# Attention with two gated MLPs on one core: the order of the first loads, the rest scores and the warm-up products

## The chip, the cores and the metric

One core of a Trainium2 chip runs the whole program. The metric is the device time of one execution in microseconds; lower is better. The engines are TensorE (PE, with its weight loads as PEld), VectorE (DVE), ScalarE (ACT), GpSimd (POOL) and SyncE (SP, which issues nearly all transfers here). PE writes into PSUM, from where ACT and DVE read. Each engine works through its own instructions in program order.

## What is computed

Three stages follow one another; all inputs and outputs are float32 or wider. Only the first is touched by the change.

```python
# q, k, v: (4 batches, 12 heads, 448, 64)
scores = scale * q @ k.T - log(448)
attn = 1 / (1 + exp(-scores))             # a sigmoid, no row sum
x = attn @ v                              # heads side by side: (4, 448, 768)
x = moe(x, ...)                           # gated MLP: in 768 -> 1024, over positions, out 512 -> 768
out = moe2(x, ...)                        # the second gated MLP
```

## The kernel before

The attention part treats the 48 heads in 12 groups of four (`attention`, L318). A group's q and k are loaded as 128 partitions (four heads by 32 rows t), each with 14 consecutive positions c of 64 values (`load_qk`, L323). DVE turns 32x32 blocks of them so that the 64 values of a head lie on 32 partitions in two halves (`turn`, L363): `tq` from q, `tk` from the first 12 positions of k, `tr` from the last two. So a group's 448 keys fall into three blocks of 128 and a rest of 64. For the three blocks each operand is split into a rounded part and what remains (`high` and `low`), and a score block (`scores`, L442) is three products by two halves by four heads, 24 in all. Block (0,0), the very first, is made of unsplit operands and uses two value banks beside one score buffer, so that it can start early.

The rest keys of two groups n and n+1 share a block (`scores_rest`, L469): it needs `tq` and `tr` of both groups, unsplit, and its sigmoid goes into one tile for both.

A score block takes two of the three buffers of `ps_att` (two PSUM banks each). ACT weighs them (`weigh`, L435: sigmoid, one instruction for a pair of heads) into a tile that is the moving operand of the value products (`values`, L490), with the stationary operand from `vt` (blocks) or `vr` (rests). A group's values for a pair x of heads add up over its four blocks in one bank, and `gather` (L504) copies the sum away on DVE when the last is in.

The values are loaded by `load_v` (L332): `vt` holds the 12 first positions of the rows t, three positions per block of 32 partitions, for four heads; four DMAs, one per 32 partitions. `vr` (L349) holds the rests, four DMAs more.

The order of work is written out by hand. `units` (L530) lists the score blocks; the loop at L575 issues at step s block s and then the value products that `sums` names for the step. For a pair of groups n, m the order is (n,0), (n,1), (n,3), (n,2), (m,0), (m,1), (m,2), where 3 is the rest of both groups; for the first pair L537 swaps it to (0,0), (0,1), (0,2), (0,3), and the rest is then the last of group 0's value products (`last_of`, L487). At step 0 group 1 is turned (L581). At steps 3 and 6 a later group is turned, at steps 0 and 4 ACT makes the rounded parts of a group (`high`), at 1 and 5 DVE makes the remainders (`low`). `belt.tick` (L589) moves the weight conversions on by a stage each: a load by SP, five operations on DVE (L170 to L188), a cast on ACT (L201), a difference on DVE (L203). In the first steps the first conversion's DVE part is issued at step 1 and its cast at step 2, behind that step's sigmoids.

Ahead of the loop (L565 to L574) stand the loads of groups 0 and 1, products of an identity with itself that keep PE at work while the loads run (L573), and the turning of group 0.

Of the kernel before, what the change touches and what calls it, by code (L numbers as in the profile page):

```python
# [26 lines left out]
def tile_sigmoid_attention_two_gated_mlps(  # L27
# [32 lines left out]
    nc = tc.nc  # L60
    B, H, S, D = q.shape
# [6 lines left out]
    TC = S // 32  # L68
# [30 lines left out]
    def av_bank():  # L99
        return ps_av.tile([P, 512], F32, tag="av", name="av")  # L100
# [217 lines left out]
    def attention(apool, epool, ps_att, done):  # L318
        G = H // 4
        NG = B * G  # L320
        raws, turned, ops, vs, att, avp = {}, {}, {}, {}, {}, {}

        def load_qk(n, xs="kq"):  # L323
            b, i = divmod(n, G)
            hs = slice(4 * i, 4 * i + 4)
            for x in xs:
                t = apool.tile([P, TC * D], F32, tag=f"in{x}", name=f"in{x}", bufs=2)
                src = {"k": k, "q": q}[x][b, hs].rearrange("h (t c) d -> (h t) (c d)", c=TC)
                nc.sync.dma_start(out=t, in_=src)
                raws.setdefault(n, {})[x] = t  # L330

        def load_v(n):  # L332
            b, i = divmod(n, G)
            vs[n] = vt, vr = (
                epool.tile([P, 4, 3, D], F32, tag="v", name="vt", bufs=3),
                epool.tile([P, 2, D], F32, tag="vr", name="vr", bufs=3),
            )
            src = v[b, 4 * i:4 * i + 4].rearrange("h (t c) d -> t h c d", c=TC)
            for e in range(4):
                ts = slice(32 * e, 32 * e + 32)  # L340
                nc.sync.dma_start(
                    out=vt[ts].rearrange("p h c d -> p h (c d)"),
                    in_=src[:, :, 3 * e:3 * e + 3].rearrange("t h c d -> t h (c d)"),
                )
            later["rows"] = lambda: load_v_rest(n, vr, src)
            if n > 0:
                later.pop("rows")()

        def load_v_rest(n, vr, src):  # L349
            for e in range(4):  # L350
                ts = slice(32 * e, 32 * e + 32)
                h = 2 * ((e // 2 + n) % 2)
                hs = slice(h, h + 2)
                nc.sync.dma_start(out=vr[ts], in_=src[:, hs, 12 + e % 2])

        def turn_keys(tk, k):
            for j in range(2):
                nc.vector.transpose(
                    out=tk[:, j].rearrange("p (c e) t -> p c e t", c=3),
                    in_=k[:, j, :12].rearrange("p (e c) d -> p c e d", c=3),  # L360
                )

        def turn(n):  # L363

            tk = apool.tile([P, 2, 12, 32], F32, tag="tk", name="tk", bufs=1)
            tr = apool.tile([P, 2, TC - 12, 32], F32, tag="tr", name="tr", bufs=2)
            tq = apool.tile([P, 2, TC, 32], F32, tag="tq", name="tq", bufs=2)
            at = raws.pop(n)
            k, q = [at[x].rearrange("p (c j d) -> p j c d", c=TC, j=2) for x in "kq"]
            turned[n] = [t.rearrange("p j c t -> p (j c t)") for t in (tk, tr, tq)]  # L370
            ops[n] = (
                apool.tile([P, 2, 6 * P], F32R, tag="opk", name="opk", bufs=2),
                apool.tile([P, 2, 2 * S], F32R, tag="opq", name="opq", bufs=2),
            )
            if n > 1:
                turn_keys(tk, k)
                nc.vector.transpose(out=tq, in_=q)
                nc.vector.transpose(out=tr, in_=k[:, :, 12:])
                return
            if n == 1:  # L380
                nc.vector.transpose(out=tq, in_=q)
                high(n, (1,), nc.vector.tensor_copy)
                low(n, (1,))
                nc.vector.transpose(out=tr, in_=k[:, :, 12:])
                turn_keys(tk, k)
                high(n, (0,), nc.vector.tensor_copy)
                low(n, (0,))
                return

            def some_k(r):  # L390
                nc.vector.transpose(out=tk[:, :, 4 * r:4 * r + 4], in_=k[:, :, r:12:3])
                return 0, slice(r * P, (r + 1) * P)

            def some_q(j):
                nc.vector.transpose(out=tq[:, j], in_=q[:, j])
                return 1, slice(0, S), slice(j, j + 1)

            qs = some_q(0), some_q(1)
            for x in qs:
                high_part(n, *x)  # L400
            for j in range(2):
                nc.vector.transpose(out=tk[:, j, :4], in_=k[:, j, :12:3])
            ks = some_k(1), some_k(2)
            for x in ks:
                high_part(n, *x)
            for x in qs + ks:
                low_part(n, *x)
            nc.vector.transpose(out=tr, in_=k[:, :, 12:])
# [7 lines left out]
        def high_part(n, i, cols, js=slice(0, 2), copy=nc.scalar.copy):  # L416
            t, hi, _ = views(n, i, cols, js)
            copy(out=hi, in_=t)

        def low_part(n, i, cols, js=slice(0, 2)):  # L420
            t, hi, lo = views(n, i, cols, js)
            nc.vector.tensor_tensor(out=lo, in0=t, in1=raw(hi), op=ALU.subtract)

        def high(n, parts=(0, 1), copy=nc.scalar.copy):
            for i in parts:
                high_part(n, i, slice(0, (3 * P, S)[i]), copy=copy)

        def low(n, parts=(0, 1)):
            for i in parts:
                low_part(n, i, slice(0, (3 * P, S)[i]))  # L430
# [53 lines left out]
            att[n, 3] = att[n + 1, 3] = a = epool.tile([P, 4, S], F32, tag="ar", name="ar", bufs=1)  # L484
            weigh(a, pairs(sc))

        def last_of(n):  # L487
            return 2 if n else 3

        def values(n, r, x):  # L490
            if r == 0:
                avp[n, x] = av_bank()
            vt, vr = vs[n]
            at = REST * ((x + n) % 2)
            ps = slice(at, at + REST)
            for o in range(2):
                h = 2 * x + o
                nc.tensor.matmul(  # L498
                    avp[n, x][o * D:(o + 1) * D, :S],
                    vt[:, h, r] if r < 3 else vr[ps, o], att[n, r][:, h] if r < 3 else att[n, r][ps, h],  # L500
                    start=(r == 0), stop=(r == last_of(n)),
                )

        def gather(n, x):  # L504

            b, i = divmod(n, G)
            y = chunk_of(b, 2 * i + x)
            o = avp.pop((n, x))[:, :S].rearrange("p (c t) -> p t c", c=TC)

            def back(at, t0, t1, c0=0, c1=TC):  # L510
                dst = y[:, at:at + (t1 - t0) * (c1 - c0)]
                nc.vector.tensor_copy(
                    out=dst.rearrange("p (t c) -> p t c", t=t1 - t0), in_=o[:, t0:t1, c0:c1]
                )

            if b % 2 == 0:
                back(0, 0, 32)
            else:
                t, c = divmod(3 * P, TC)
                back(SPAN, 0, t)  # L520
                back(SPAN + t * TC, t, t + 1, 0, c)
                back(S, t, t + 1, c, TC)
                back(S + TC - c, t + 1, 32)
# [3 lines left out]
        units, sums = [], {}  # L527
        for n in range(0, NG, 2):
            m, at = n + 1, len(units)
            units += [(n, 0), (n, 1), (n, 3), (n, 2), (m, 0), (m, 1), (m, 2)]  # L530
            both = lambda n, r: [(n, r, 0), (n, r, 1)]
            todo = (
                [(n, 0, 0)], [(n, 0, 1), (n, 1, 0)], [(n, 1, 1)] + both(n, 3), both(n, 2),
                both(m, 0), both(m, 3) + [(m, 1, 0)], [(m, 1, 1), (m, 2, 0)], [(m, 2, 1)],
            )
            if n == 0:
                units[2:4] = units[3:1:-1]  # L537
                todo = [both(0, r)[::-1] for r in range(4)] + list(todo[4:])
            for s, x in enumerate(todo, at + 1):
                sums.setdefault(s, []).extend(x)  # L540
        U = len(units)
# [17 lines left out]
        def weigh_up(s):  # L559
            for n, r, x in sums.get(s, ()):  # L560
                values(n, r, x)
                if r == last_of(n) and n < NG - 1:
                    gather(n, x)

        load_qk(0, "qk")  # L565
        load_qk(1, "q")
        load_v(0)
        load_qk(1, "k")
        later.pop("rows")()
        belt.tick(1)  # L570
        warm = av_bank()
        for _ in range(10):
            nc.tensor.matmul(warm[:, :P], ident, ident, start=True, stop=True)  # L573
        turn(0)  # L574
        for s in range(U + 2):  # L575
            p, step = divmod(s, 7)
            score(s)
            weigh_up(s)
            n = 2 * p + (1 if step < 2 else 2 if step < 6 else 3)
# [10 lines left out]
            if step in (0, 4):  # L590
                n = 2 * p + 2 + step // 4
# [516 lines left out]
```

## Time and profile before

| | us |
|---|---|
| median of 3 runs (lowest, highest) | 556.52 (556.45, 557.28) |
| the profiled execution, its own time | 556.21 |
| its span, first to last instruction | 554.4 |
| PE busy | 549.1 |
| DVE busy | 368.1 |
| ACT busy | 231.5 |

The rows below come from that one profiled execution; times in them are from the start of its span. PE records overlap, since products are pipelined, so a block's own length is the distance to the next block in the chain. "Idle before" is time in which the engine did nothing ahead of an instruction, with what released it. "issue" is time in which the engine waited for nothing that the profile shows. In the table of stretches, the DMA share is the mean busy share of the core's 16 DMA engines; packets in flight together can bring it above 1.

### The profile page before, as it was taken

The numbers are of one execution on the slowest core, as the hardware profiler recorded it, in microseconds if no ns is written. First come the engines' busy times: TensorE is split into PE (matmuls) and PEld (weight loads), VectorE is DVE, ScalarE is ACT, GpSimd is POOL, SyncE is SP. The second block draws the span as 40 slices with busy tenths as digits, with TensorE's granted clock in tenths as the row PEclk, the third lists the DMA queues.
The fourth block names the chain that finished last, engine by engine and source line by source line (L and its number), as shares of the span: only waits on it lengthen the run. The fifth ranks groups of instructions, "written<-read, shape, count | busy, mean of one in ns | idle before, by whom it ended". The sixth has DMA issues, their size and how long they took to land.

```text
span 554.4 us, 9199 instructions
## 1 busy us (share of the span) xinstructions
PE 549.1 (99%) x3472; PEld 437.0 (79%) x3472; DVE 368.1 (66%) x839; ACT 231.5 (42%) x388; POOL 32.7 (6%) x62
## 2 busy tenths in 40 slices
PE   8999999999999999999999999999999999999997
PEld 6444444444799898898998889998999899989886
DVE  6879999997689699999864977951542264224311
ACT  5778778786353262361443156310320041113101
POOL 0000000000110100300100011000100020011000
PEclk9999999999999999999999999999999999999999
DMA  7777677653044265453445534200400032003003
GB/s 246 195 175 224 191 211 200 159 109 73 2 135 141 62 169 120 121 148 102 145 153 129 147 112 125 70 0 9 78 14 0 9 58 36 1 15 60 11 1 114
DMA packets 96892, 56.45 MB, mean 102 GB/s; under 512 B 67536, under 2 KB 84048, under 8 KB 96848
## 3 DMA queue, kind: packets, MB, share of 16 engines
q1 hardware_dynamic: 96704, 55.60, 38.7%
q8 instruction: 27, 0.44, 0.4%
q10 hardware_dynamic: 144, 0.26, 0.1%
q14 instruction: 17, 0.14, 0.1%
HBM read 44.83 MB, written 11.01 MB: 101 GB/s over the span
## 4 chain that ended last, share of the span: by engine, by line
PE 98%; DMA 1%; SPq 0%; issue 0%; DVE 0%
PE t L685 17%; PE t L639 17%; PE av L498 13%; PE sc L771 10%; PE sc L461 9%; PE t L705 6%; PE av L771 5%; PE av L705 3%; PE sc L705 3%; PE sc L781 3%; PE t L867 3%; PE av L867 3%; PE sc L479 2%; PE av L781 2%; PE t L781 2%; DMA vt<-in_v_dram 1%
## 5 line engine op out<-in xcount | busy, mean ns | idle before, releaser
L437 ACT ACTIVATE a<-sc,small 128x896 f32<-128x896 f32 x71 | 67.7, 1008 | 20.4 <-PE sc L461 20.4
L498 PE MATMUL av<-a,vt 128*64 128x448 f32 x288 | 62.9, 553 | 0.4 <-DMA vt<-in_v_dram 0.4
L648 DVE BATCH_NORM_STATS2 st<-vr 128x6 f32<-128x512 f32 x28 | 19.4, 694 | 65.7 <-ACT vr L645 65.7
L461 PEld LDWEIGHTS sc<-opq,opk 32*128 32x128 f32 x840 | 38.6, 183 | 25.5 <-issue 10.8
L645 ACT ACTIVATE vr<-t 128x512 f32<-128x512 f32 x28 | 16.7, 598 | 92.3 <-PE t L639 88.5
L461 PE MATMUL sc<-opq,opk 32*128 32x448 f32 x840 | 53.3, 380 | 0.0
L498 PEld LDWEIGHTS av<-a,vt 128*64 128x64 f32 x288 | 17.2, 136 | 32.4 <-issue 27.9
L639 PE MATMUL t<-vh,xh 128*128 128x512 f32 x112 | 41.5, 391 | 0.0
L715 DVE SCALAR_TENSOR_TENSOR gt<-t,bb 128x448 f32<-128x448 f32 x16 | 10.9, 682 | 45.5 <-PE t L705 45.5
L723 ACT CAST gh<-u 128x448 fp32r<-128x448 f32 (+1 forms) x16 | 8.6, 540 | 71.5 <-DVE u L719 71.5
L650 POOL TENSOR_SCALAR st<-st 128x1 f32<-128x1 f32 x28 | 11.0, 391 | 466.6 <-DVE st L649 466.6
L639 PE MATMUL t<-vh,xl 128*128 128x512 f32 x98 | 38.1, 389 | 0.0
L685 PE MATMUL t<-xh,uh 128*128 128x448 f32 x96 | 34.8, 363 | 0.0
L685 PE MATMUL t<-xh,ul 128*128 128x448 f32 x96 | 34.8, 362 | 0.0
L685 PE MATMUL t<-xl,uh 128*128 128x448 f32 x96 | 34.6, 360 | 0.0
L705 PE MATMUL t<-sh,v 128*128 128x448 f32 x112 | 32.8, 362 | 0.0
L639 PE MATMUL t<-vl,xh 128*128 128x512 f32 x84 | 32.7, 389 | 0.0
L182 DVE SCALAR_TENSOR_TENSOR f<-w,f 128x256 uint32<-128x256 uint32 x72 | 30.7, 426 | 2.5
L188 DVE SCALAR_TENSOR_TENSOR f<-w,f 128x256 int32<-128x256 int32 x72 | 30.6, 425 | 2.4
L685 PE MATMUL t<-xh,vl 128*128 128x448 f32 x96 | 29.7, 363 | 0.0
L177 ACT ACTIVATE g<-w 128x256 f32<-128x256 f32 x48 | 20.1, 432 | 19.4 <-DMA w<-in_moe_w_out_dram 9.7
L667 ACT CAST v<-vr 128x512 fp32r<-128x512 f32 x24 | 14.9, 621 | 30.6 <-DVE vr L659 30.6
(211 smaller groups left out, 1291.2 us busy)
## 6 DMA issues: line engine op xcount, KB each, us to landing
w<-in_moe_w_in_dram SPq DMA_DIRECT2D x48, 256.0 KB, 3.5
w<-in_moe_w_out_dram SPq DMA_DIRECT2D x24, 256.0 KB, 3.0
inq<-in_q_dram SPq DMA_DIRECT2D x12, 448.0 KB, 6.4
ink<-in_k_dram SPq DMA_DIRECT2D x12, 448.0 KB, 5.7
vt<-in_v_dram SPq DMA_DIRECT2D x48, 96.0 KB, 6.1
out_dram<-y SPq DMA_DIRECT2D x48, 56.0 KB, 1.9
flat<-f SPq DMA_DIRECT2D x18, 128.0 KB, 1.7
w<-flat SPq DMA_DIRECT2D x12, 192.0 KB, 2.4
```

The source lines that it names most:

```text
L177: nc.scalar.activation(g, high.bitcast(F32), AF.Square)
L182: nc.vector.scalar_tensor_tensor(out=f.bitcast(U32), in0=low.bitcast(U32), scalar=29, in1=f.bitcast(U32), op0=ALU.logical_shift_right, op1 ...
L188: nc.vector.scalar_tensor_tensor(out=f, in0=high, scalar=-0x40000000, in1=f, op0=ALU.bitwise_and, op1=ALU.bitwise_or)
L437: nc.scalar.activation(a[:, dst], src[..., :S], AF.Sigmoid, bias=bias_s, scale=scale)
L461: nc.tensor.matmul(banks[h][:, :S], opk[ps, x, o:o + P], opq[ps, y, S * j:S * (j + 1)], start=(t == 0), stop=(t == len(todo) - 1), tile_po ...
L498: nc.tensor.matmul(avp[n, x][o * D:(o + 1) * D, :S], vt[:, h, r] if r < 3 else vr[ps, o], att[n, r][:, h] if r < 3 else att[n, r][ps, h], ...
L639: nc.tensor.matmul(ps[:, :FF], a, w, start=(c == 0 and n == 0), stop=(c == self.kc - 1 and n == 2),)
L685: nc.tensor.matmul(ps[:, :S], w, a, start=(c == 0 and n == 0), stop=(c == self.kc - 1 and n == 2),)
L705: nc.tensor.matmul(ps[:, :S], a, w, start=(n == 0), stop=(n == len(todo) - 1))
L771: nc.tensor.matmul(self.o[m][:, :n_cols], w, a, start=(not second and i == 0 and n == 0), stop=(second and i == KF - 1 and n == 2),)
L781: nc.tensor.matmul(ps[:, :cols.stop - cols.start], a, w, start=(not second and i == 0 and n == 0), stop=(second and i == KF - 1 and n == 2),)
L867: nc.tensor.matmul(ps[:, :FF], x, w[:, c], start=(c == 0 and n == 0), stop=(c == KD - 1 and n == 2),)
```

## The change

The four value DMAs of a group go by head instead of by 32 partitions: each fills all 128 partitions with 768 bytes of one head, read from four strided pieces of 32 rows. The first loads are issued in the order q0, k0, values of 0, q1, k1, rests of 0. In the first pair of groups the rest scores take the third place, as in all other pairs, and the third key block the fourth; the value products follow, so that block 2 is the last of group 0 too and `last_of` goes. Turning group 1 makes all transpositions first, and then the rounded parts and remainders of q and of k. There are eleven identity products in place of ten.

```diff
@@ -335,13 +335,13 @@
                 epool.tile([P, 4, 3, D], F32, tag="v", name="vt", bufs=3),
                 epool.tile([P, 2, D], F32, tag="vr", name="vr", bufs=3),
             )
+            for h in range(4):
+                src = v[b, 4 * i + h].rearrange("(t c) d -> t (c d)", c=TC)[:, :12 * D]
+                nc.sync.dma_start(
+                    out=vt[:, h].rearrange("p c d -> p (c d)"),
+                    in_=src.rearrange("t (e f) -> e t f", e=4),
+                )
             src = v[b, 4 * i:4 * i + 4].rearrange("h (t c) d -> t h c d", c=TC)
-            for e in range(4):
-                ts = slice(32 * e, 32 * e + 32)
-                nc.sync.dma_start(
-                    out=vt[ts].rearrange("p h c d -> p h (c d)"),
-                    in_=src[:, :, 3 * e:3 * e + 3].rearrange("t h c d -> t h (c d)"),
-                )
             later["rows"] = lambda: load_v_rest(n, vr, src)
             if n > 0:
                 later.pop("rows")()
@@ -379,12 +379,11 @@
                 return
             if n == 1:
                 nc.vector.transpose(out=tq, in_=q)
-                high(n, (1,), nc.vector.tensor_copy)
-                low(n, (1,))
                 nc.vector.transpose(out=tr, in_=k[:, :, 12:])
                 turn_keys(tk, k)
-                high(n, (0,), nc.vector.tensor_copy)
-                low(n, (0,))
+                for x in (1, 0):
+                    high(n, (x,), nc.vector.tensor_copy)
+                    low(n, (x,))
                 return
 
             def some_k(r):
@@ -484,9 +483,6 @@
             att[n, 3] = att[n + 1, 3] = a = epool.tile([P, 4, S], F32, tag="ar", name="ar", bufs=1)
             weigh(a, pairs(sc))
 
-        def last_of(n):
-            return 2 if n else 3
-
         def values(n, r, x):
             if r == 0:
                 avp[n, x] = av_bank()
@@ -498,7 +494,7 @@
                 nc.tensor.matmul(
                     avp[n, x][o * D:(o + 1) * D, :S],
                     vt[:, h, r] if r < 3 else vr[ps, o], att[n, r][:, h] if r < 3 else att[n, r][ps, h],
-                    start=(r == 0), stop=(r == last_of(n)),
+                    start=(r == 0), stop=(r == 2),
                 )
 
         def gather(n, x):
@@ -534,8 +530,7 @@
                 both(m, 0), both(m, 3) + [(m, 1, 0)], [(m, 1, 1), (m, 2, 0)], [(m, 2, 1)],
             )
             if n == 0:
-                units[2:4] = units[3:1:-1]
-                todo = [both(0, r)[::-1] for r in range(4)] + list(todo[4:])
+                todo = [both(0, r)[::-1] for r in (0, 1, 3, 2)] + list(todo[4:])
             for s, x in enumerate(todo, at + 1):
                 sums.setdefault(s, []).extend(x)
         U = len(units)
@@ -559,17 +554,16 @@
         def weigh_up(s):
             for n, r, x in sums.get(s, ()):
                 values(n, r, x)
-                if r == last_of(n) and n < NG - 1:
+                if r == 2 and n < NG - 1:
                     gather(n, x)
 
         load_qk(0, "qk")
-        load_qk(1, "q")
         load_v(0)
-        load_qk(1, "k")
+        load_qk(1, "qk")
         later.pop("rows")()
         belt.tick(1)
         warm = av_bank()
-        for _ in range(10):
+        for _ in range(11):
             nc.tensor.matmul(warm[:, :P], ident, ident, start=True, stop=True)
         turn(0)
         for s in range(U + 2):
```

## Rows read from the trace of the kernel before

**Rows 1.** The page: PE's busy time, and the chain that ended last by engine.
```profile
PE 549.1 (99%) x3472; PEld 437.0 (79%) x3472; DVE 368.1 (66%) x839; ACT 231.5 (42%) x388; POOL 32.7 (6%) x62
...
PE 98%; DMA 1%; SPq 0%; issue 0%; DVE 0%
```

**Rows 2.** The chain in order of time: start us, us, what.
```profile
9.60 1.72 PE av L498 x8
...
14.40 1.69 PE sc L479 x32
...
16.09 1.65 PE av L498 x8
...
17.75 1.43 PE sc L461 x20
...
19.18 0.91 PE av L498 x8
...
20.09 1.74 PE sc L461 x19
...
23.49 1.71 PE sc L461 x19
...
27.01 1.42 PE sc L461 x21
...
49.19 1.42 PE sc L461 x21
```

**Rows 3.** Timeline of PE: start us, us, line, operation, tiles, forms, count, idle before.
```profile
1.35 4.63 PE L573 MATMUL av<-ident 128*128 128x128 f32 x20 [1.35 <-POOL ident masks.py:199]
...
6.18 0.69 PE L461 MATMUL sc<-tq,tk 32*128 32x448 f32 x2 [0.20 <-DVE tk L402]
...
17.68 0.48 PE L461 MATMUL sc<-opq,opk 32*128 32x448 f32 x4
...
20.02 0.47 PE L461 MATMUL sc<-opq,opk 32*128 32x448 f32 x2
```

**Rows 4.** PE's waits over the span: total us, times, longest us.
```profile
PE av L498 <- DMA vt<-in_v_dram: 0.4, 1, 0.4
```

**Rows 5.** Timeline of ACT, 8 to 23.6 us.
```profile
16.23 0.41 ACT L201 CAST vh<-f 128x256 fp32r<-128x256 f32 x1 [1.53 <-DVE f L188]
...
16.54 1.91 ACT L437 ACTIVATE ar<-sc,small 128x896 f32<-128x896 f32 x2
...
19.28 1.91 ACT L437 ACTIVATE a<-sc,small 128x896 f32<-128x896 f32 x2 [0.84 <-PE sc L461]
```

**Rows 6.** Timeline of DVE, 3 to 16.3 us.
```profile
4.03 1.17 DVE L395 STREAM_TRANSPOSE tq<-inq 128x448 f32<-128x448 f32 x2 [3.15 <-DMA inq<-in_q_dram]
...
5.81 0.51 DVE L402 STREAM_TRANSPOSE tk<-ink 128x128 f32<-128x128 f32 x2 [0.61 <-DMA ink<-in_k_dram]
...
8.83 1.07 DVE L381 STREAM_TRANSPOSE tq<-inq 128x896 f32<-128x896 f32 x1
...
15.77 0.42 DVE L188 SCALAR_TENSOR_TENSOR f<-w,f 128x256 int32<-128x256 int32 x1
```

**Rows 7.** Timeline of SP, the queue that issues the loads.
```profile
2.10 2.03 SPq L341 DMA_DIRECT2D vt<-in_v_dram  x4
...
8.76 0.43 SPq L162 DMA_DIRECT2D w<-in_moe_w_in_dram  x1
```

**Rows 8.** Stretches: us; busy of PE, PEld, DVE, ACT, POOL; clock, DMA share, GB/s.
```profile
1.50:5.00 3.50, 3.50 (x17) 3.50 (x18) 0.97 (x2) 0.99 (x3) 0.00 (x0) 1.00 0.91 322
...
5.00:5.50 0.50, 0.50 (x4) 0.50 (x4) 0.20 (x1) 0.50 (x2) 0.00 (x0) 1.00 1.00 403
...
5.50:6.00 0.50, 0.48 (x3) 0.18 (x1) 0.19 (x1) 0.30 (x1) 0.00 (x0) 1.00 0.96 328
...
6.00:6.50 0.50, 0.32 (x4) 0.32 (x8) 0.50 (x3) 0.00 (x0) 0.00 (x0) 1.00 1.16 260
...
27.00:49.20 22.20, 22.20 (x246) 10.41 (x244) 17.51 (x42) 17.31 (x23) 0.00 (x0) 1.00 0.73 190
```

## The prediction

> **What bounds the kernel now.** I read the page's busy table and its chain first: TensorE (PE) is busy for 549.1 of 554.4 us, and PE makes up 98% of the chain that ended last, DMA 1% [rows 1]. So only a change in when PE works can move the time, and PE sits idle for little more than 5 us in all, most of it before the first and after the last product. Next the chain in order of time over the first 27 us [rows 2]: from 9.60 us on PE goes from one block to the next without a gap. A full score block of four heads takes 1.43 us, a block of four value products 1.65, the rest scores 1.69, the rest values 0.91. Two score blocks stand out, 1.74 at 20.09 and 1.71 at 23.49: 0.3 us more each for the same products. The PE timeline tells why [rows 3]: at 20.02 two products start instead of four, and the other heads begin 0.3 us later. They wait for a score buffer. There are three (ps_att, two banks each), a block takes two, and ScalarE (ACT) must weigh what is in them first. The release comes 1.06 us after ACT starts on a pair (19.28 to 20.34), so 1.16 after the last score, while the rest values between the two blocks last only 0.91. PE's one named wait in this stretch is 0.4 us for the values of group 0 [rows 4]. Last come ACT and VectorE (DVE) [rows 5, 6], since both work in program order, and SP with the transfers [rows 7, 8].
>
> Times below are of the profiled execution: span 554.4, its own time 556.21, which is 0.3 below the median of the three runs, 556.52.
>
> **The change, part by part.**
>
> *The loads of group 0.* SP issues q0, k0, the four value loads, then q1, k1. The values start about 0.5 us earlier at SP (the four take 2.03 us from 2.10 on now [rows 7]), q1 moves from just ahead of them to about 3.7, and k1 and all behind it keep their places. The data moves in order: from 1.5 to 5.0 us 1127 KB (3.5 us at 322 GB/s), so q0 and k0 (917 KB) are through at about 4.5 and the values follow [rows 8].
>
> What the new value load costs no row shows. It moves the same bytes (393 KB in pieces of 768 B), but its source is an outer count of 4 pieces against 128 partitions, while every load of before has 32 or 128 as the outer count on both sides. If the pieces are dealt to all sixteen DMA engines, the lower bound is the rate at the start of the values, 328 GB/s [rows 8]: 1.2 us. If they are dealt by the outer count that both sides share, only four engines work. One busy engine moved 328/(16 x 0.96) = 21.4 GB/s there, 260/(16 x 1.16) = 14.0 in the next half microsecond, 25.2 with the large pieces of q and k before. Four engines then need 4.6 us (3.9 to 7.0). I take four at 21.4: a source of 4 and a destination of 128 have no finer outer cut in common. The Trainium skill (DMA: Bandwidth & Descriptors, "Why a DMA increments its semaphore by 16 and not by 1") says that a DMA runs on the largest number of engines up to 16 that divides both slowest dimensions: 4 here, so the rule gives the sum I take; no load in this trace tests it. Against it the skill (SBUF — State Buffer, "Door 1: The DMA port swizzle") says that a transfer into 32 partitions reaches half of the ports and one into 128 all; the trace agrees (403 GB/s for q and k, 260 among the values), and by this alone the load gets cheaper and the sum is that of the first rival.
>
> On those four engines the values end at 4.5 + 4.6 = 9.1, a sixteenth of q1 (28.7 KB at 25.2 GB/s, 1.1 us) at 10.2, of k1 at 11.35. The first load landed 0.7 us after its bytes were through (458 KB at about 3.3, VectorE starts on it at 4.03 [rows 6]); with that lag q1 lands at 10.9 and k1 at 12.05. The values land near 9.8: PE's wait for them stays, 0.2 us longer. The order by head does not help, as heads 2 and 3 are used first and loaded last.
>
> *VectorE.* The nine operations of turn(1) are the same, in another order: tq, the rests tr, the keys, then the copies and differences. They run without a gap from 8.83 on now, and the first weight conversion, right behind them, is done at 16.19 [rows 6]. With q1 there at 10.9, tq ends at 11.97, and tr starts at 12.1 where it would at 9.9: everything behind is late by **2.2 us**, the conversion done at 18.4. Its own input does not set this: SP issues it at 8.76 [rows 7], and behind q1 and k1 (through at 11.35) its 16 KB per engine are there by 13, long before VectorE comes to it.
>
> *Rest scores third.* The same products, so PE's busy time is the same; what moves is who waits for a buffer. The blocks become (0,0), (0,1), rest, (0,2), (1,0). The rest needs tq and tr of group 1, now 12.4 instead of 11.2: PE loses about 0.6 there, after the part that needs only group 0. The short rest values now stand ahead of (1,0), so that block has the buffer wait: its second buffer is free 1.06 us after ACT starts on (0,2). On ACT that pair stands behind one cast of L201, which waits for the conversion on VectorE. Today the same cast holds up the rest scores' pair (16.23, then 16.54 [rows 5]), behind which a full value block of 1.65 hides it. That cover is gone: the short values hide 0.91. So (1,0) gets its second buffer at 18.4 + 0.04 (to the cast) + 0.31 (to the weighing) + 1.06 = 19.8.
>
> From there I add blocks: (1,0) ends at 19.8 + 1.49 = 21.3 (1.49 is what the block at 20.09 took from its own release at 20.34 [rows 2, 3]), values 22.95, (1,1) without its wait 24.4, values 26.05, (1,2) without its wait 27.45. Before, that block ended at 25.20 [rows 2]: **2.25 us later**. The two removed waits (0.6) are in this sum, and PE runs without gaps from there to the end, so nothing is won back. A longer or shorter value wait in group 0 is swallowed by the wait at (1,0).
>
> *The eleventh identity product and last_of.* Ten products are 20 records about 0.22 us apart, ending at 5.98, and PE idles 0.20 before the first score [rows 3]. Two records more fill that gap and cost 0.05 to 0.25; it too ends in the wait at (1,0), so nothing. The granted clock is 1.00, the 2.4 GHz level, in every stretch [rows 8], so there is none to win. last_of only fixes which product closes the sum.
>
> The sum: 556.21 + 2.25 = **558.5**. Bounds: the four engines' 3.9 to 7.0 us move it by -0.7 to +2.4; a lag of 0.1 to 1.3 instead of 0.7 (k0: through at 4.5, landed before 5.8 [rows 6]) by -0.6 to +0.6; together, both ends at once being unlikely, +0.9 to +4.
>
> **The rivals.**
>
> *All sixteen engines carry the load* (not slower). q1 lands before 8.8, VectorE has no gap, the conversion is done at 16.19 as now. Values start 0.24 earlier (after ACT's first pair). The buffer wait at (1,0) still comes: ACT starts on (0,2) at 16.54, release 17.60, while PE arrives at 16.73 (9.36 + 1.65 + 1.69 + 1.65 + 1.43 + 0.91 and some hundredths); (1,0) ends at 19.09 against 19.18, values 20.74, (1,1) 22.17, values 23.83, (1,2) 25.26 against 25.20. So +0.1 (-0.75 if the cast is out of the way, +0.6 if q1 is a little late): 556.3, from 555.5 to 556.8. For it speak the fall in rate among 32-partition loads; against it the outer count of 4. It decides if q1 lands before 9 us.
>
> *Four engines, and later loads late too.* Per group those engines then carry 4.6 us of values, 2.3 of q and k, 1.6 of weights (five per pair of groups), 0.2 of rests: 8.7 of the 11.1 us that a group lasts (from group 2's first score block at 27.01 to group 4's at 49.19 are two [rows 2]). At 14.0 GB/s the values alone take 7.0 and the engines are full: from there loads fall behind and PE waits in most groups, 0.3 to 0.5 us in ten of them, 3 to 5 us more: 562. Against it speaks that the mean DMA share of that stretch is 0.73 [rows 8], so that there is room on the engines that the values leave.
>
> **How the numbers follow.** Four engines 0.64, sixteen 0.28, four with late loads 0.08. About 0.2% (1.1 us) is what a measurement of this kernel can tell from no change. Of the first case I give 0.09 to less than that; so slower is 0.64 - 0.09 + 0.07 = 0.62, same 0.09 + 0.26 + 0.01 = 0.36, faster 0.02. The range takes the four-engine case to +3.9 (560.1) and most of the sixteen-engine case (556.2); the likeliest case alone is 557.1 to 560.1.
>
> **What would show it.** In the changed profile: a DMA share near 0.25 for some 4 us from about 5 us on, q1's transposition starting at 10 or later instead of 8.83, the cast of L201 past 18, (1,0) split into two starts with a gap of 2 us, (1,1) and (1,2) at 1.43 without the split start. If the share stays near 1 while the values load and tq starts at 8.83, the first rival holds. If the value rows of later groups show PE waiting for vt, the second.

## The result and the profile after

The changed kernel takes **559.88 us** (559.53 to 560.91, 6 runs); the kernel before, measured beside it, 556.75 (556.45 to 558.56, 6 runs). The ratio is 1.0053 [1.0038, 1.0068], so 0.5% slower. The profiled execution took 559.84 us with a span of 558.1; before it was 556.21 and 554.4. So 3.6 to 3.7 us were lost between the two profiles, and 3.1 between the medians, where 2.25 were forecast.

The page gives the first reading: PE's busy time, and the shares of the chain that ended last.

```profile
PE 550.9 (99%) x3474; PEld 438.2 (79%) x3474; DVE 368.0 (66%) x839; ACT 231.2 (41%) x388; POOL 32.6 (6%) x62
...
PE 96%; DMA 1%; DVE 1%; SPq 1%; ACT 0%; issue 0%
```

PE is still the bound, but 4% of the chain, some 20 us, now belongs to others, against 2% in [rows 1]. PE's waits over the span, apart from 1.3 us for the identity at the start that both kernels have (total us, times, longest us):

```profile
PE sc L460 <- ACT a L436: 1.0, 1, 1.0
PE av L494 <- ACT a L436: 0.8, 1, 0.8
PE av L494 <- DMA vt<-in_v_dram: 0.5, 1, 0.5
```

All three lie in the first 22 us, and they are new or longer than the 0.4 of [rows 4]. The chain in order of time (start us, us, what) shows how they hang together:

```profile
5.57 8.08 DMA ink<-in_k_dram
...
13.67 0.03 DVE tr L382
...
19.36 0.43 DVE f L188
...
19.82 0.41 ACT vh L201
20.22 0.92 ACT a L436
...
21.18 1.50 PE sc L460 x17
...
24.33 1.43 PE sc L460 x21
...
27.41 1.44 PE sc L460 x18
28.85 1.81 PE av L494 x12
```

Read from the end: the scores of (1,2) are done at 28.85, where they were done at 25.20 (23.49 + 1.71) in [rows 2], 3.65 us later; that is the whole loss of the span, so nothing is won or lost behind it. (1,1) and (1,2) take 1.43 and 1.44: the two buffer waits of [rows 2] are gone. (1,0) waits for ACT's weighing (20.22), that for the cast of L201 (19.82), that for the conversion on DVE, and DVE turned q1 late (its row follows) and then waited another 0.1 us for a k1 that landed 8.08 us after its issue. PE, from the first values to (1,0) (start us, us, line, operation, tiles, forms, count, idle before):

```profile
10.10 0.94 PE L494 MATMUL av<-a,vt 128*64 128x448 f32 x2 [0.82 <-ACT a L436]
11.57 1.69 PE L494 MATMUL av<-a,vt 128*64 128x448 f32 x6 [0.54 <-DMA vt<-in_v_dram]
13.19 2.58 PE L478 MATMUL sc<-tq,tr 32*64 32x448 f32 x32
...
19.69 0.47 PE L460 MATMUL sc<-opq,opk 32*128 32x448 f32 x2
21.18 1.50 PE L460 MATMUL sc<-opq,opk 32*128 32x448 f32 x22 [1.03 <-ACT a L436]
```

The value products come a head at a time, two records each. The first start at 10.10. The row names ACT, but the pair that they read was weighed by 9.19 (ACT's two instructions of 8.03 us, 1.16 together), so I read the wait as one for the values of head 2; head 3, loaded last, keeps PE until 11.57. The rest scores' row is 2.58 long, where the timeline of before has 1.76 for them (at 14.34): the rest keys of group 1 are turned only at 13.67 + 0.31. At 19.69 two products of (1,0) start, and the other heads 1.5 us later. DVE and SP tell why, here q1's transposition on DVE:

```profile
12.44 1.11 DVE L381 STREAM_TRANSPOSE tq<-inq 128x896 f32<-128x896 f32 x1 [4.25 <-DMA inq<-in_q_dram]
```

and the loads at SP:

```profile
1.63 2.48 SPq L340 DMA_DIRECT2D vt<-in_v_dram  x4
4.15 1.38 SPq L329 DMA_DIRECT2D inq<-in_q_dram  x1
5.57 0.43 SPq L329 DMA_DIRECT2D ink<-in_k_dram  x1
```

VectorE idles 4.25 us for q1, where it had no gap in [rows 6]. SP's issue of q1 alone took 1.38 us, against 0.39 to 0.43 for the other three q and k loads of groups 0 and 1. Last the stretches (us; busy of PE, PEld, DVE, ACT, POOL; clock, DMA share, GB/s):

```profile
4.50:6.50 2.00, 2.00 (x13) 1.88 (x16) 2.00 (x7) 1.63 (x4) 0.00 (x0) 1.00 0.28 75
6.50:8.00 1.50, 1.50 (x23) 1.25 (x20) 1.50 (x5) 0.19 (x1) 0.00 (x0) 1.00 0.89 209
27.00:49.20 22.20, 22.20 (x244) 10.37 (x240) 17.68 (x40) 17.32 (x23) 0.00 (x0) 1.00 0.67 210
```

From 4.5 to 6.5 us the share is 0.28, close to 4 of 16 engines, at 75 GB/s, where [rows 8] show 0.96 to 1.16 and 260 to 403 GB/s for the half microseconds from 5 to 6.5. Then q1 and k1 fill the other engines.

### The profile page after: what moved, and what is told of

Read it like the earlier page. It is cut to its first block, busy times and chain, and to the rows that moved or that the text cites. A ratio compares the mean times of both kernels' runs of the same rounds, so it can differ in the third digit from the quotient of the medians.

```text
span 558.1 us, 9192 instructions
## 1 busy us (share of the span) xinstructions
PE 550.9 (99%) x3474; PEld 438.2 (79%) x3474; DVE 368.0 (66%) x839; ACT 231.2 (41%) x388; POOL 32.6 (6%) x62
## 4 chain that ended last, share of the span: by engine, by line
PE 96%; DMA 1%; DVE 1%; SPq 1%; ACT 0%; issue 0%
PE t L679 17%; PE t L633 17%; PE av L494 12%; PE sc L765 10%; PE sc L460 8%; PE t L699 6%; PE av L765 5%; PE av L699 3%; PE sc L699 3%; PE sc L775 3%; PE t L861 3%; PE av L861 3%; PE sc L478 2%; PE av L775 2%; PE t L775 1%; DMA ink<-in_k_dram 1%
## 5 line engine op out<-in xcount | busy, mean ns | idle before, releaser
L639 ACT ACTIVATE vr<-t 128x512 f32<-128x512 f32 x28 | 16.7, 598 | 92.5 <-PE t L633 88.7
L709 DVE SCALAR_TENSOR_TENSOR gt<-t,bb 128x448 f32<-128x448 f32 x16 | 10.9, 682 | 45.6 <-PE t L699 45.6
L644 POOL TENSOR_SCALAR st<-st 128x1 f32<-128x1 f32 x28 | 10.9, 390 | 470.3 <-DVE st L643 470.3
L177 ACT ACTIVATE g<-w 128x256 f32<-128x256 f32 x48 | 19.8, 432 | 17.4 <-DMA w<-in_moe_w_out_dram 9.5
```

Of the source, the lines that this page charges most:

```text
L177: nc.scalar.activation(g, high.bitcast(F32), AF.Square)
```

## The experiments

The ratios are against runs of the kernel before on the same chip, which had medians of 557.48, 557.37 and 557.28 in the three sets of experiments.

**1. The changed kernel with the value load of before.**

```diff
-            for h in range(4):
-                src = v[b, 4 * i + h].rearrange("(t c) d -> t (c d)", c=TC)[:, :12 * D]
+            src = v[b, 4 * i:4 * i + 4].rearrange("h (t c) d -> t h c d", c=TC)
+            for e in range(4):
+                ts = slice(32 * e, 32 * e + 32)
                 nc.sync.dma_start(
-                    out=vt[:, h].rearrange("p c d -> p (c d)"),
-                    in_=src.rearrange("t (e f) -> e t f", e=4),
+                    out=vt[ts].rearrange("p h c d -> p h (c d)"),
+                    in_=src[:, :, 3 * e:3 * e + 3].rearrange("t h c d -> t h (c d)"),
                 )
-            src = v[b, 4 * i:4 * i + 4].rearrange("h (t c) d -> t h c d", c=TC)
```

> The changed kernel with the value loads of before (32 partitions each); order of loads, rest third, eleven products as changed. Theory (the value load runs on four of the sixteen DMA engines and q1 and k1 of those engines wait behind it): the stretch from 5 to 6.5 us is back at 250 to 330 GB/s with a DMA share near 1, q of group 1 is turned by 9 us in place of 12.44, the conversion ahead of the cast is done by 16.5 in place of 19.79, and the 3.1 us are gone: 556.4 to 557.2, within 0.5 us of the kernel before. Rival (the place of the rest scores and the order of the loads cost the time, whatever the load's shape): block (1,0) still stalls by over 1 us and the time stays at 559 or more. A stall of about 0.9 us at (1,0), paid back by the two waits that are gone at (1,1) and (1,2), is expected by the theory too.

Measured: 556.62 us, ratio 0.9992 [0.9976, 1.0009], span 554.0. Two stretches, and PE's rows around the first values and (1,0):

```profile
5.00:6.50 1.50, 1.18 (x14) 0.82 (x16) 1.01 (x5) 0.74 (x3) 0.00 (x0) 1.00 1.15 247
4.50:6.50 2.00, 1.68 (x17) 1.32 (x20) 1.51 (x6) 1.18 (x3) 0.00 (x0) 1.00 1.12 265
```

```profile
8.86 2.01 PE L494 MATMUL av<-a,vt 128*64 128x448 f32 x8
...
16.47 0.47 PE L460 MATMUL sc<-opq,opk 32*128 32x448 f32 x2
17.13 1.49 PE L460 MATMUL sc<-opq,opk 32*128 32x448 f32 x22 [0.19 <-ACT a L436]
```

The share is 1.15 with this load, and 1.12 over the two microseconds in which the changed kernel had 0.28. The values wait for nothing, and start 0.74 us earlier than in [rows 2] (9.60). The loss is gone with the load's shape; the order of the issues and the place of the rest cost nothing that shows. A stall of 0.66 us at (1,0) is left.

**2. The kernel before with the new value load alone** (the same replacement the other way round, order of issues as before).

> The kernel before with the value load by head and nothing else; q of group 1 is still issued ahead of the values. Theory: again a share near 0.25 for some 4 us while the values load, but q of group 1 is through before it, so VectorE starts its transposition near 9; the values land some 1.5 to 2 us late (11 to 11.5 in place of 9.46) and PE waits for them, with k of group 1 late behind them; 1.5 to 2.5 us slower than before, 558.2 to 559.3. Rival (the load's shape costs nothing in itself): within 0.5 us of the kernel before, and a share near 1 in that stretch.

Measured: 560.32 us, ratio 1.0051 [1.0036, 1.0066], span 557.5: the load alone gives the loss of the whole change, a little over what was expected. The stretch of few engines, and PE's wait:

```profile
6.00:7.50 1.50, 1.50 (x12) 0.98 (x16) 1.50 (x5) 0.73 (x2) 0.00 (x0) 1.00 0.27 89
```

```profile
PE av L498 <- DMA vt<-in_v_dram: 2.2, 2, 1.8
```

The share is 0.27 here too, later than in the changed kernel because q1 is ahead. The price shows at another place: with values behind q1, PE waits 2.2 us for them.

**3. The changed kernel, group 0 loaded as before, later groups by head.**

```diff
+            if n == 0:
+                for e in range(4):
...
+            else:
+                for h in range(4):
...
```

> The changed kernel with the value load of group 0 as before and those of the eleven later groups by head. Theory (only the first group's load is on the path): 556.4 to 557.2, as with all loads as before, and no PE wait on vt after 12 us. Rival (the four engines that carry the values are full over the whole attention part, and PE pays in later groups): 1.5 us or more above the kernel before, with PE waits on vt or turned operands in later groups.

Measured: 556.36 us, ratio 0.9979 [0.9965, 0.9993], span 554.2. PE's waits, and the stretch of two later groups:

```profile
PE av L575 <- POOL ident masks.py:199: 1.3, 1, 1.3
PE sc L468 <- ACT a L444: 0.3, 1, 0.3
```

```profile
27.00:49.20 22.20, 22.20 (x244) 10.41 (x244) 17.54 (x41) 17.45 (x22) 0.00 (x0) 1.00 0.68 206
```

No wait for vt, although eleven groups are loaded by four engines each. So the slow load costs only where something is late for it: at the start. The rival "four engines, and later loads late too" falls.

**4. Sixteen engines by the order of the source alone.** The destination is unchanged, and the source is read as 32 rows of four pieces; the value rows then stand on other partitions than the keys, so the value products pair other rows, in the same number and sizes.

```diff
-                    in_=src.rearrange("t (e f) -> e t f", e=4),
+                    in_=src.rearrange("t (e f) -> t e f", e=4),
```

> The changed kernel with one thing turned round in the source of the value load: 32 rows of four pieces in place of four pieces of 32 rows, the same bytes, the same 768 byte pieces and the same 128 partitions. (The rows of the values then stand at other partitions than the keys, so the value products pair other rows; their number and size are the same.) Theory (engines are dealt by the outermost count that both sides share, 16 of 32 and 128, against 4 of 4 and 128): share near 1 and 330 GB/s or more while the values load, they are through by about 6, q of group 1 lands before 8.8, the time is 556.0 to 557.0. Rival (loads into all partitions by head are slow for another reason, such as the number of pieces or the ports): share near 0.25 as in the changed kernel, 559 or more.

Measured: 556.84 us, ratio 0.9999 [0.9988, 1.0009], span 554.6. The first half microsecond in which the values load, the next, and the whole stretch in which the changed kernel had a share of 0.28:

```profile
4.50:5.00 0.50, 0.50 (x4) 0.50 (x4) 0.50 (x2) 0.38 (x1) 0.00 (x0) 1.00 1.04 352
5.00:5.50 0.50, 0.50 (x4) 0.50 (x4) 0.11 (x1) 0.50 (x2) 0.00 (x0) 1.00 0.69 229
...
4.50:6.50 2.00, 1.97 (x13) 1.68 (x12) 1.05 (x5) 1.09 (x2) 0.00 (x0) 1.00 0.84 245
```

Same pieces, same partitions, same bytes, and the share is 0.84 at 245 GB/s in place of 0.28 at 75. It starts at 1.04 but does not stay there, and the 330 GB/s expected hold for the first half microsecond only. Only the outer count of the source differs, and with it the order in which the pieces are read and the partitions that they go to. That the load was slow by its count of four is the reading that forecast a share of 4/16 before the run. Pieces of 768 bytes and gaps between them are no rival, since the old load has them too (experiment 1).

**5. The cast out of ACT's way**: the kernel of experiment 1, with the weight conversion one step later.

```diff
-            belt.tick(rate(p, step))
+            if s:
+                belt.tick(rate(p, step))
```

> The run with the value loads of before in the changed kernel, and the weight conversions not moved on at step 0, so that the first cast on ScalarE stands behind the pair of (0,2) in place of ahead of it; VectorE's order is the same. Theory (the stall of 0.66 us at (1,0) is ScalarE's queue: the cast waits for the conversion and the pair waits for the cast): ScalarE starts on (0,2) 0.1 us after its last score, the stall shrinks to about 0.25 (1.16 to the release against 0.91 of rest values), the span is 0.4 us shorter than with the cast ahead, and the time some 0.8 below the kernel before: a ratio near 0.9985. Rival (the buffer is late for another reason, such as the length of the sigmoids alone): the stall stays at 0.6 or more and nothing is gained.

Measured: **555.84 us**, ratio 0.9963 [0.9948, 0.9979], span 554.0. ACT's rows and PE's (1,0):

```profile
16.01 1.91 ACT L436 ACTIVATE a<-sc,small 128x896 f32<-128x896 f32 x2 [1.12 <-PE sc L460]
17.80 0.40 ACT L201 CAST vh<-f 128x256 fp32r<-128x256 f32 x1
```

```profile
16.80 1.76 PE L460 MATMUL sc<-opq,opk 32*128 32x448 f32 x24
```

The pair of (0,2) is weighed ahead of the cast, and (1,0) runs through in 1.76 instead of being split. The gain is more than the 0.9985 expected; 8 of the 31 executions of the kernel before in this set, and none of the 8 of this kernel, have the lower mean clock told of in the last section. This kernel beats the kernel before and the changed one: its median is lower by 1.5 us than that of the kernel before beside it, and by 4.0 than that of the change, taken in another set. The profiled span is no shorter than that of experiment 1, since k0 landed 0.33 us later in this execution (first score at 6.25 instead of 5.92).

**6. The order by head kept, on sixteen engines**: the source order of experiment 4, with the keys transposed into the same order, so that the whole computation is done, and the later cast.

```diff
-                    in_=src.rearrange("t (e f) -> e t f", e=4),
+                    in_=src.rearrange("t (e f) -> t e f", e=4),
...
+            def turned_block(j, r):
+                return tk[:, j, 4 * r:4 * r + 4].rearrange("p c t -> p (c t)").rearrange("p (t e) -> p e t", e=4)
...
-                nc.vector.transpose(out=tk[:, :, 4 * r:4 * r + 4], in_=k[:, :, r:12:3])
+                for j in range(2):
+                    nc.vector.transpose(out=turned_block(j, r), in_=k[:, j, r:12:3])
...
+            if s:
+                belt.tick(rate(p, step))
```

> The load with 32 rows of four pieces, the keys turned into the same order (VectorE's transpositions write with a step of four, and group 0's two key blocks take two instructions each), so that the result is the reference's, and the later cast. Theory: the load costs what it did with 32 rows of four pieces, VectorE's transpositions keep their 0.5 us, and the time is that of the run with the value loads of before and the later cast, within 0.5 us. Rival (the step of four makes the transpositions of the keys dear): each of them takes 0.8 us or more in place of 0.53, VectorE's chain after 9 us is over 1 us longer, the conversion later by that, and the time at the kernel before or above it.

Measured: 556.24 us, ratio 0.9972 [0.9960, 0.9985], span 553.9. VectorE's transpositions of k1:

```profile
10.72 1.57 DVE L358 STREAM_TRANSPOSE tk<-ink 128x384 f32<-128x384 f32 x2
```

The two with the new order take 1.57 us instead of 0.99 for the pair in experiment 1. So the theory was wrong that they keep their 0.5 us each, but PE waits for nothing behind them, and the time is 0.4 us above experiment 5. The change's idea, a load by head over all partitions, thus does work once the source's outer count is 32; against the old load in its place (experiment 5) it gains nothing that shows.

**7. The rest scores third, alone** (in the kernel before, with the order of turning that goes with it).

> The kernel before with the rest scores third and the order within turning group 1, and nothing else: loads and their order as before, ten products. Theory: the rest's place is worth little either way: the two waits of 0.3 us at (1,1) and (1,2) go, a stall of 0.6 to 0.9 us at (1,0) comes, PE's wait of 0.4 us for the values stays; a ratio of 0.9990 to 1.0010. Rival (the place of the rest is what costs in the changed kernel): 1.5 us or more slower.

Measured: 557.64 us, ratio 0.9996 [0.9982, 1.0010], span 556.6. In the profiled execution PE waited 1.9 us ahead of its first value products. The row names the rests' load, which these products do not read; I take it as a wait for the values, as in [rows 4]. What follows is in no row of before. PE, and a stretch behind the wait:

```profile
10.51 2.02 PE L494 MATMUL av<-a,vt 128*64 128x448 f32 x8 [1.90 <-DMA vr<-in_v_dram]
12.46 3.09 PE L478 MATMUL sc<-tq,tr 32*64 32x448 f32 x32
```

```profile
11.80:15.20 3.40, 3.40 (x36) 0.86 (x32) 3.33 (x6) 0.00 (x0) 0.00 (x0) 0.50 0.89 328
```

The granted clock is 0.50, the 1.2 GHz level, for 3.4 us, and the rest scores take 3.09 us. The removed buffer waits are worth nothing that the median shows.

**8. Eleven products alone**: the kernel before with `range(11)`.

> The kernel before with eleven identity products in place of ten. Theory: the eleventh ends at 6.2 to 6.4 us, where PE waited for the first keys; the first score starts at most 0.25 us later, and the time does not change: 0.9995 to 1.0010. Rival (it matters for what the first scores run at): the first score products take another time than the 0.69 us of the kernel before, and the ratio leaves that range.

Measured: 556.88 us, ratio 0.9978 [0.9963, 0.9993], a gain where none was expected. The profiled execution does not show it: there PE waited 1.8 us ahead of the values, and the span is 555.7. The interval overlaps with that of the unchanged kernel in experiment 10, so this settles nothing.

**9. q1 and k1 ahead of the values**: the changed kernel with the two lines of loads exchanged.

```diff
-        load_v(0)
         load_qk(1, "qk")
+        load_v(0)
```

> The changed kernel with q1 and k1 issued ahead of the values of group 0, which still go by head: nothing large stands behind the values now. This measures the four-engine load by itself. Theory (four engines, whose rate falls only while the other twelve carry q1 and k1): VectorE turns group 1 without a gap from about 9 and the rests by 10.3; the values start at about 6.7, the share stays near 0.25 for 4.6 to 5.5 us (17 to 21 GB/s for each of four engines) and they land at 11.5 to 12.5, PE waits 2 to 3 us for them, the conversion is done by 16.5, and the kernel is 1.5 to 3 us slower than before. Rival (q1's late landing in the changed kernel came from q1 itself, not from the values ahead of it): q of group 1 lands after 11 here too.

Measured: 561.30 us (560.60 to 561.57, 5 runs), ratio 1.0064 [1.0042, 1.0086], span 558.8, worse than expected. A stretch in which the values load and one behind PE's wait, then PE's row and VectorE's wait for k1:

```profile
7.50:8.00 0.50, 0.50 (x15) 0.45 (x11) 0.50 (x2) 0.19 (x1) 0.00 (x0) 1.00 0.35 132
...
12.30:15.70 3.40, 3.40 (x8) 0.87 (x6) 2.94 (x7) 0.00 (x0) 0.00 (x0) 0.50 0.91 328
```

```profile
11.94 4.15 PE L494 MATMUL av<-a,vt 128*64 128x448 f32 x8 [2.89 <-DMA vt<-in_v_dram]
```

```profile
9.41 0.31 DVE L382 STREAM_TRANSPOSE tr<-ink 128x128 f32<-128x128 f32 x1 [0.21 <-DMA ink<-in_k_dram]
```

With q1 and k1 out of the way VectorE has no gap beyond 0.3 us, and the price moves to PE: 2.9 us without work for the values, and then the same fall to 0.50 for 3.4 us, in which eight value products take 4.15. PE has the values some 4.5 us after q1 and k1 are through (at about 7.4, an estimate: by 7.0 us 5.5 x 309 = 1.70 of 1.835 MB were moved). That estimate is rough, since VectorE waited for k1 until 9.41, so this run gives no time of the four-engine load by itself. One busy engine moved 132/(16 x 0.35) = 23.6 GB/s from 7.5 to 8.0.

**10. The kernel before once more**, as a control in the same set.

> The kernel before, unchanged, as a second look at how long PE waits for the values of group 0 and as a measure of what the comparison can tell: a ratio of 0.9985 to 1.0015. If the place of the values behind q1 makes their landing uncertain, as the two runs with that order suggest (PE's first value product at 10.5 and 10.8 in place of 9.6), this profile's lies between 9.4 and 11; the rival, that 9.6 is fixed and the eleventh product or the rest's place moved it, gives 9.6 within 0.1.

Measured: 557.25 us, ratio 0.9996 [0.9979, 1.0012]: no difference, with an interval 0.0033 wide that the other results are to be held against. Its profiled execution is no evidence on when values land: PE came to them at 9.73 and found them there.

**11. The best kernel with ten products.**

```diff
-        for _ in range(11):
+        for _ in range(10):
```

> The run with the value loads of before and the later cast, with ten identity products in place of eleven. Theory: the first keys land at 5.8 to 6.3, after ten as after eleven products, so the time is the same: a ratio to the kernel before within 0.0010 of the 0.9963 with eleven. Rival (the eleventh keeps the clock up): a granted clock under 1.00 somewhere between 5 and 9 us or slower first scores, and over 0.5 us more.

Measured: 555.69 us (555.05 to 557.80, 12 runs), ratio 0.9967 [0.9952, 0.9982]: no different from 0.9963 with eleven. Yet its profiled execution took 557.8, and the first score block tells where:

```profile
6.58 1.12 PE L460 MATMUL sc<-tq,tk 32*128 32x448 f32 x2 [0.60 <-DVE tk L401]
...
8.24 0.95 PE L460 MATMUL sc<-tq,tk 32*128 32x448 f32 x2
```

Here these products take 1.12 and 0.95 us, against 0.65 and 0.54 with eleven in experiment 5.

## Why the prediction was right, and where it was off

**The shape of the load.** Right. Four engines: share 0.28 in the changed kernel and 0.27 with the load alone, and 0.84 over the same two microseconds as soon as the outer count is 32. That bears out the rule of the Trainium skill (DMA: Bandwidth & Descriptors, "Why a DMA increments its semaphore by 16 and not by 1"), which no load of before tested. The rival of sixteen engines fell with it; what it forecast for them, +0.1 us, or -0.75 with the cast out of the way, is near what the profiled spans give: +0.2 in experiment 4, the load by head on sixteen engines, and -0.4 in experiments 1 and 5, with the start 0.33 later in the second of them. What that rival rested on does not show: by the same stretch the load into all 128 partitions on sixteen engines (245 GB/s, experiment 4) is no faster than the loads into 32 (265, experiment 1). So the fall to 260 in [rows 8], which the prediction took as a sign of it, is not shown to come from the 32 partitions.

**Its price.** The time came out near the upper end of the range. The term that was mis-sized is the 4.6 us of the values on four engines, and with it "q1 lands at 10.9". It landed at 12.44, and k1 at 13.65 instead of 12.05. From there the sum kept its distances:

| | forecast | measured |
|---|---|---|
| q1 there | 10.9 | 12.44 |
| tr starts | 12.1 | 13.67 |
| conversion done | 18.4 | 19.79 |
| (1,0) gets its second buffer | 19.8 | 21.18 |
| (1,2) ends | 27.45 | 28.85 |

All lines are late by 1.4 to 1.6. 2.25 + 1.4 = 3.65, the measured distance at (1,2). The values were to land near 9.8; PE had the last of them at 11.57. Taking 0.7 us of lag off, they were through at 10.87, some 6.4 us after 4.5 (an estimate), which is inside the prediction's bounds of 3.9 to 7.0. The 21.4 GB/s per engine did not hold even at first: 75/(16 x 0.28) = 16.7 from 4.5 to 6.5. Those 2 us moved 150 of the 393 KB, and the remaining 243 KB took 4.4 us on four engines, 13.9 GB/s each, close to the 14.0 that the prediction kept as a bound. Why the rate fell is open. Traffic on the other engines was not tried by itself, and it does not explain the 16.7, which came while they did little; in like stretches experiments 2 and 9 show 89/(16 x 0.27) = 20.6 and 23.6.

The sum also missed that q1 begins late on the twelve free engines. Its bytes there, 12/16 of it, do not show before 6.5 us (share 0.28), while its issue at SP took 1.38 us and ended at 5.53. With the load alone k1, next behind the values, took 2.25 us to issue. Why a load behind these is slow to issue, and idle engines stay idle beside them, is open.

**VectorE and the cast.** Right: the conversion was late by the same as q1, and the cast, ahead of (0,2)'s pair on ACT, held (1,0). Experiment 5 shows the cast to be the link in the kernel of experiment 1: with it later, the stall of 0.66 at (1,0) is gone without any change of the loads. The changed kernel with the later cast was not run, and the cast is not all of its loss. That kernel reaches (1,0) at 19.69, experiment 1 at 16.47: 3.2 of the 4.1 us between these two profiles were lost ahead of that block, most of it in the waits for the values and the rest keys. The longer stall (1.49 against 0.66) adds 0.8.

**"A longer or shorter value wait in group 0 is swallowed."** Right as to the end of (1,0), though the wait itself was 0.82 + 0.54 us in place of the 0.6 forecast: these and 0.8 more in the rest scores stand ahead of (1,0), where PE still waited 1.03. The gap between the two starts was forecast as 2 and is 1.5, since PE itself came later.

**The two removed buffer waits.** Right: 1.43 and 1.44 at (1,1) and (1,2), and with the old load (1,0) has a wait instead (0.66 in experiment 1). Alone, in experiment 7, the new place brings no gain that the median shows; its profile does not tell why, since PE was late there by the wait for the values.

**Four engines with later loads late.** It fell, as experiment 3 shows; the share from 27 to 49.2 us is 0.68 there, and 0.67 in the changed kernel.

**The eleventh product costs nothing.** No loss shows. Whether it is a gain is open: alone it gave 0.9978, in the best kernel 0.9963 against 0.9967. The prediction put the clock at 1.00 ahead of the first scores, and for that the product durations are the better witness: the clock column shows 1.00 in the execution whose first products took 1.12 us, too.

**What the prediction did not see** is that the new order of issues may be a gain by itself (last section): experiment 3 has it and gave 0.9979 [0.9965, 0.9993], experiment 1 has it too and gave 0.9992 with 1 inside the interval. In the changed kernel the load's shape covered it.

## What to carry to other kernels

Before changing how a load is cut, write down the outermost count on both sides: here 4 against 128 left twelve of sixteen DMA engines idle, and exchanging two axes of the source took it back (experiments 4 and 6). A slow load costs where a consumer is late: eleven of twelve by-head loads were free, and the one at the start cost 3 us, by PE's own waits and by a chain of q1, VectorE's order, one cast on ACT and a score buffer. With that chain out of the way (experiment 9) PE's wait for the values and the lower clock behind it cost 4 us. When a sum rests on a rate, carry the whole spread of the rates that the rows show: 21.4 GB/s was taken, 14.0 stood in the next row, and 16.7 and 13.9 came.

## What was not expected of the hardware

**The clock after a wait.** In the kernel before the values follow q1, and PE's first value products began at 9.60, 9.73, 10.51 and 10.82 us in four profiles of that order with the old load. PE's idle time ahead of them is 1.9 us in experiment 7 and 2.9 with q1 and k1 first; behind both the granted clock is 0.50 for 3.4 us. Behind 1.8 us of idle time in the profiles of experiments 2 and 8 it stayed at 1.00. Over all executions, the mean granted clock was 0.997 or lower in 20 of 94 of the kernel before (the control included), in 4 of 22 of experiments 7 and 8, whose values follow q1 too, in 2 of 62 of the six kernels with the values ahead of q1 and the load of group 0 on sixteen engines (experiments 1, 3 to 6 and 11), in 1 of 6 of the changed kernel, in 4 of 6 with the load by head alone, and in 5 of 5 with q1 and k1 first. In the kernel before the executions at the lower mean have a median of 559.3 us, the others 557.2. So loading the values ahead of q1 seems to spare some executions about 2 us; the kernel before with that order alone was not run.

**The first products.** With eleven identity products the first score took 0.64 to 0.69 us in all eight profiles; with ten it took 0.65 or 0.69 in two and 1.12 in three. That fits the medians only weakly, as told above, and stays open.
